# Three of fifteen streamed weight slices loaded as 108 and 20 rows

## The chip, the cores and the metric

The kernel runs on one core of a Trainium2 chip. Five engines work side by side on the core: PE (TensorE, the matmuls), ACT (ScalarE), DVE (VectorE), POOL (GpSimd) and SP (SyncE, which here only issues transfers). Sixteen DMA engines move data between the memory outside the core (HBM) and the on-chip memory (SBUF, 128 rows or "partitions"). The metric is the device time of one execution in microseconds (us); less is better. The median of three runs is given with the lowest and the highest.

## The reference, cut to what matters

Two attention layers work on the same input `x` of 2048 tokens by 640 features, and a gate per token mixes them. Layer A is recurrent: it takes the tokens in 64 segments of 32, puts 8 memory rows ahead of each, and the first 8 rows of its output are the memory of the next segment.

```python
for s in range(n_seg):                                  # 64 segments, one after the other
    h = jnp.concatenate([mem, xs], axis=1)              # 8 + 32 rows of 640
    q = jnp.einsum('btd,dhe->bhte', h, Wq)              # 32 heads of 192: 640 x 6144 weights
    k = jnp.einsum('btd,dhe->bhte', h, Wk)
    v = jnp.einsum('btd,dhe->bhte', h, Wv)
    ...                                                 # masked softmax over the 40 rows
    o = jnp.einsum('bhte,hed->btd', o, Wo)              # 6144 x 640 weights
    mem = o[:, :M, :].copy()
...
return g * a + (1 - g) * b                              # b: local dilated attention, not recurrent
```

So every segment needs all of `Wq`, `Wk`, `Wv` and `Wo` (31.5 MB in bf16), which is more than the on-chip memory holds, and no segment can start before the one ahead of it has its output.

## The kernel before

The kernel has three stages. `part_b` computes layer B and the gate (up to about 163 us of the span). `prepass` computes what of layer A does not depend on the memory (up to about 459 us). `part_a` then runs the 64 segments, and `part_z` finishes some output rows from 1880 us on.

**Slices.** The weights are cut into 80 slices of 128 rows by 1536 columns (384 KB): `("q", R, kc)`, `("k", R, kc)`, `("v", R, kc)` with R from 0 to 3 and kc from 0 to 4, and `("oa", i)` and `("ob", i)` for `Wo`. `weights_setup` (L339) spreads `N_STREAM = 15` of them evenly over an estimated segment; those are streamed, that is, loaded again in each segment. The other 65 stay in SBUF. In the order of use the streamed ones are q02, k04, q14, q20, k20, q30, k30, v0 (R 0, kc 0), v1, v2, v3, oa0, oa5, oa7 and ob4, where q14 stands for `("q", 1, 4)`.

**Loads.** `get_slice` (L390) gives back a resident tile, or calls `load_slice` (L374) for a tile of the pool `wstream`, tag `wst`, which has `WBUFS = 5` buffers. `load_slice` makes one transfer on SP's queue: from the weight itself (L382) or, for the four streamed slices of `Wo`, from a copy `wscr` in HBM that was rearranged once at the start (L380). A buffer's load can be issued when the matmuls on the slice five ahead of it are done. The scheduler of the framework puts the waits on semaphores in; for PE and ACT the order written out in `part_a` is kept (`manual_schedule`, L519). Transfers issued by SP and ACT take their completion semaphore in turn out of eight, and a transfer is issued only when the one that used its semaphore before has landed.

**A segment.** `m_qk` (L523) multiplies the 40 rows by a `q` or `k` group: five slices, four matmuls each, side by side on the columns of PE (L531). `t_qk` transposes (L545), `s_a` and `s_b` make the scores (L568, L577), `e_exp` and `e_norm` the softmax, `m_v` the values (L614), `pv_half` the weighted sum (L634, L638), `o_group` the product with `Wo` (L671), and `sel` (L681) picks the memory rows for the next segment. At the segment's end ACT copies the last results of `pv_half` (L644, L649), issues the next segment's loads `KZ` (L504) and `ZQ` (L505) and the store `oz_dram` (L732), and then copies the first part of the output (L739), from which `sel` starts the next memory. ACT issues four more transfers per segment: the store of the output rows (L764, 4 rows outermost), `Vz` (L510), `a4` (L715) and `hT` (L500). SP issues the 15 slices and nothing else there.

The 15 slices and these seven are the 22 transfers of a segment. `prepass` reads slices too; q14 and v0 are each streamed once more there. At the very end ACT stores the last segment's rows in four transfers of 24 rows (L767). In `part_b` the weight `wo_pad` is loaded in four transfers of 20 rows (L136).

Of the kernel before, what the change touches and what calls it, by code (L numbers as in the profile page):

```python
# [15 lines left out]
N_LATE = 55  # L16
N_LATE2 = 22
WBUFS = 5

_DEV = {"mode": "full"}  # L20

# [3 lines left out]
class _K:  # L25
# [313 lines left out]
    def weights_setup(self):  # L339
        nc, tc = self.nc, self.tc  # L340
        keys = self.slice_keys()
        gap = {("q", 0, 3): 200, ("k", 0, 3): 0, ("q", 1, 0): 620, ("k", 1, 0): 270, ("q", 2, 0): 570, ("k", 2, 0): 270,
               ("q", 3, 0): 980, ("k", 3, 0): 270, ("v", 0, 0): 690, ("v", 1, 0): 270, ("v", 2, 0): 710,
               ("v", 3, 0): 1160, ("oa", 6): 1530, ("q", 0, 0): 200}
        at, t = {}, 0
        for k in keys:
            t += gap.get(k, 0)
            at[k] = t
            t += 163
        self.stream_keys = set()  # L350
        for i in range(N_STREAM):
            left = [k for k in keys if k not in self.stream_keys]
            self.stream_keys.add(min(left, key=lambda k: abs(at[k] - (i + 0.5) * t / N_STREAM)))
        rest = [k for k in keys if k not in self.stream_keys]
        first = ["q", "k", "v", "oa", "ob"]
        self.late = sorted(rest, key=lambda k: first.index(k[0]))[-N_LATE:]
        self.wres = self.ctx.enter_context(tc.tile_pool(name="wres", bufs=1))
        self.res_tiles = {}
        self.wscr = {}
        self.early = [k for k in rest if k not in self.late]  # L360
        self.wstream = self.ctx.enter_context(tc.tile_pool(name="wstream", bufs=WBUFS))

# [11 lines left out]
    def load_slice(self, pool, key, name, tag=None):  # L374
        src, split = self.slice_info(key)
        kw = {"tag": tag} if tag else {}
        t = pool.tile([128, 1536], BF, name=name, **kw)
        v = t if split is None else t.rearrange("p (c f) -> p c f", c=split[0])
        if key in self.wscr:
            self.nc.sync.dma_start(t[:], self.wscr[key])  # L380
        else:
            self.nc.sync.dma_start(v[:], src)  # L382
        return v

    def load_late(self, part):
# [493 lines left out]
```

## Time and profile before

| | |
|---|---|
| time, median of 3 runs | 1916.34 us (1915.34 to 1916.49) |
| the profiled execution | 1921.93 us, span 1920.1 us |
| mean granted clock of PE in it | 0.981 |
| instructions | 91,285, of PE 41,135 matmuls and as many weight loads |
| stage `part_a` | 459 to 1880 us, 64 segments of about 22.4 us |
| PE busy in that stage | 1304.9 of 1421 us |
| slices streamed | 977 transfers of 384 KB, of them 960 in the segments |
| moved in all | 489.24 MB, 423.28 MB on SP's queue, 60.12 MB on ACT's |

The profile is that of one execution. Busy time is the time in which an engine had an instruction at work. A wait is the idle time of an engine ahead of an instruction, put down to what ended it: in a line such as `PE a <- DMA b: 21.7, 1, 21.7` the three numbers are microseconds in total, the number of waits, and the longest. The chain of waits is followed back from the last instruction, each time to what released it; "issue" in it is time in which the engine waited for nothing that the profile shows, and ACTq and SPq are the times in which ACT and SP issue transfers. In the table of stages each engine has its busy time and its instructions; the granted clock of PE, the mean busy share of the 16 DMA engines and the GB/s they moved follow. The queues are q1 (issued by SP), q10 (issued by ACT), and q8 and q14, which bring instructions. Beside this the trace has a record of every packet of a DMA engine (start, length, bytes, queue) and of every increment of a semaphore; a packet there is one row of a transfer, or a 4-byte increment.

### The profile page before, as it was taken

The page shows a single profiled execution, that of the slowest core. Times are in us where ns is not written, and L with a number is a line of the kernel's source. Part 1 is how long each engine was busy: PE and PEld are TensorE (multiplying, and loading weights), DVE is VectorE, ACT ScalarE, POOL GpSimd, SP SyncE. Part 2 cuts the span into 40 slices and gives each one's busy share as a digit, 9 for nine tenths or more (in the row PEclk, how much of TensorE's full clock was granted, in tenths as well). Part 3 has the DMA queues.
Part 4 walks back from the last instruction along what each step waited for, and adds up shares of the span by engine and source line. Part 5 has one row for each costly group of instructions (what it writes and reads, how often), then busy time and mean ns, then how long its engine had stood idle before and what let it go on. Part 6 is the DMA issues. An engine that isn't in the chain of part 4 may idle for free.

```text
span 1920.1 us, 91285 instructions
## 1 busy us (share of the span) xinstructions
PE 1727.8 (90%) x41135; PEld 1023.9 (53%) x41135; DVE 651.3 (34%) x2047; ACT 742.0 (39%) x1865; POOL 70.2 (4%) x135
## 2 busy tenths in 40 slices
PE   6898899957998999999999989898999999899979
PEld 3555544424555555555555555555555555555547
DVE  4555433212333333333333333333333333333320
ACT  3666522213433333334333334333333333343340
POOL 5000000000000000000000000000000000000000
PEclk9999899988999999999999999999999999999999
DMA  6610385689989999899999889888998899998981
GB/s 167 176 31 18 112 289 152 175 280 302 300 289 287 303 289 302 284 296 293 291 293 292 286 278 303 276 286 294 294 293 286 283 298 297 296 297 286 296 291 30
DMA packets 300298, 489.24 MB, mean 255 GB/s; under 512 B 99332, under 2 KB 168452, under 8 KB 299908
## 3 DMA queue, kind: packets, MB, share of 16 engines
q1 hardware_dynamic: 183544, 423.28, 67.2%
q10 hardware_dynamic: 116364, 60.12, 11.5%
q8 instruction: 322, 5.28, 1.1%
q14 instruction: 68, 0.56, 0.1%
HBM read 448.97 MB, written 35.91 MB: 253 GB/s over the span
## 4 chain that ended last, share of the span: by engine, by line
PE 75%; ACT 8%; issue 5%; DMA 4%; ACTq 4%; DVE 3%; SPq 1%; DVEq 0%
PE ps_qk L531 24%; PE ps_v L614 12%; PE ps_wo L671 7%; PE ps_qkT L545 6%; PE ps_pre L417 6%; PE ps_bqk L220 3%; PE ps_oT L634 3%; PE ps_S L568 3%; PE ps_z L811 3%; PE ps_pre L430 2%; ACT bP L243 2%; ACT KV L536 2%; ACTq L505 1%; DVE KV L644 1%; ACT ZQ L739 1%
## 5 line engine op out<-in xcount | busy, mean ns | idle before, releaser
L536 ACT CAST KV<-ps_qk 128x384 bf16<-128x384 f32 x512 | 238.6, 479 | 397.6 <-PE ps_qk L531 389.4
L531 PEld LDWEIGHTS <-hT 128*32 128x32 bf16 x10240 | 237.4, 96 | 177.0 <-issue 59.4
L531 PE MATMUL ps_qk<-wlate_k,hT 128*32 128x384 bf16 x4352 | 247.0, 328 | 1.5 <-issue 1.5
L614 PE MATMUL ps_v<-wlate_v,hT 128*32 128x384 bf16 x4096 | 227.9, 330 | 6.3 <-issue 6.1
L671 PEld LDWEIGHTS <-KV 128*32 128x32 bf16 x6144 | 171.9, 97 | 105.2 <-DVE KV L644 35.0
L531 PE MATMUL ps_qk<-wres_q,hT 128*32 128x384 bf16 x2560 | 163.3, 329 | 20.4 <-ACT KV L536 16.8
L548 DVE COPY ZQ<-ps_qkT 128x384 bf16<-128x384 bf16 x256 | 91.0, 355 | 262.9 <-PE ps_qkT L545 262.7
L671 PE MATMUL ps_wo<-wlate_oa,KV 128*32 128x384 bf16 x2304 | 158.6, 336 | 12.8 <-DVE KV L644 2.9
L614 PEld LDWEIGHTS <-hT 128*32 128x32 bf16 x5120 | 114.5, 96 | 93.4 <-DMA wst<-in_A_Wv_dram 21.8
L531 PE MATMUL ps_qk<-wst,hT 128*32 128x384 bf16 x1792 | 153.5, 330 | 5.5 <-DMA wlate_v<-in_A_Wv_dram 4.1
L545 PE MATMUL ps_qkT<-ident,KV 128*128 128x128 bf16 x1536 | 141.2, 221 | 3.4 <-DVE ZQ L607 1.4
L671 PE MATMUL ps_wo<-wlate_ob,KV 128*32 128x256 bf16 x2688 | 133.2, 279 | 10.3 <-issue 10.2
L644 DVE CAST KV<-ps_oT 128x192 bf16<-128x192 f32 x256 | 79.8, 352 | 181.9 <-ACT KV L644 181.8
L545 PEld LDWEIGHTS <-KV 128*128 128x128 bf16 x1536 | 87.8, 98 | 94.3 <-issue 93.7
L671 PE MATMUL ps_wo<-wst,KV 128*32 128x384 bf16 (+1 forms) x1152 | 124.4, 317 | 3.2 <-issue 2.5
L644 ACT CAST KV<-ps_oT 128x192 bf16<-128x192 f32 x256 | 69.8, 325 | 119.7 <-PE ps_oT L638 118.5
L614 PE MATMUL ps_v<-wst,hT 128*32 128x384 bf16 x1024 | 89.8, 337 | 23.2 <-DMA wst<-in_A_Wv_dram 21.7
L531 PE MATMUL ps_qk<-wlate_q,hT 128*32 128x384 bf16 x1536 | 109.0, 330 | 0.3 <-issue 0.3
L618 ACT CAST KV<-ps_v 128x384 bf16<-128x384 f32 x128 | 61.2, 478 | 107.8 <-DMA wst<-wscr 33.5
L568 PE MATMUL ps_S<-ZQ,KV 128*32 128x40 bf16 (+1 forms) x4096 | 99.2, 186 | 0.5 <-DVE KV L552 0.5
L684 DVE CAST hT<-ps_mem 128x24 bf16<-128x24 f32 x126 | 22.5, 178 | 222.5 <-PE ps_mem L681 222.5
L568 PEld LDWEIGHTS <-KV 128*32 128x32 bf16 (+1 forms) x4096 | 77.5, 92 | 37.3 <-DVE KV L552 0.9
(130 smaller groups left out, 2214.3 us busy)
## 6 DMA issues: line engine op xcount, KB each, us to landing
wst<-in_A_Wv_dram SPq DMA_DIRECT2D x266, 384.0 KB
wst<-in_A_Wq_dram SPq DMA_DIRECT2D x260, 384.0 KB
wst<-wscr SPq DMA_DIRECT2D x256, 384.0 KB
wst<-in_A_Wk_dram SPq DMA_DIRECT2D x195, 384.0 KB
zpk_dram<-ZS ACTq DMA_DIRECT2D x4, 3072.0 KB
ZQ<-zpk_dram ACTq DMA_DIRECT2D x128, 96.0 KB
wlate_k<-in_A_Wk_dram SPq DMA_DIRECT2D x17, 384.0 KB
wlate_v<-in_A_Wv_dram SPq DMA_DIRECT2D x16, 384.0 KB
```

The costliest lines, as they stand in the source:

```text
L220: nc.tensor.matmul(ps[:, 0:nn], lhsT=wqk[n][:, kc, 4 * g:4 * g + 4, :].rearrange("p h d -> p (h d)"), rhs=xT[:, kc, o0:o0 + nn], start=(kc ...
L417: nc.tensor.matmul(ps[:], lhsT=sls[kc][:, c0:c0 + 128], rhs=zT[:, kc, :], start=(kc == 0), stop=(kc == KC - 1))
L531: nc.tensor.matmul(pq[32 * j:32 * j + 32, 0:384], lhsT=hT[:, kc, :], rhs=sl[:, 384 * j:384 * j + 384], start=(kc == 0), stop=(kc == KC - 1 ...
L536: nc.scalar.copy(st, pq[:, 0:384])
L545: nc.tensor.transpose(pT[:, t, :, :, :].rearrange("p j b i -> p (j b i)"), st[:, 128 * t:128 * t + 128], self.ident[:])
L548: nc.vector.tensor_copy(q_blocks(R)[:, 1:5, :, :].rearrange("p b c i -> p c b i"), pT.rearrange("p t j b i -> p (t j) b i"))
L568: nc.tensor.matmul(pSs[h][32 * j:32 * j + 32, par, 40 * r:40 * r + 40], lhsT=KT[k0:k1, 12 * r + c, :], rhs=q_blocks(R)[k0:k1, :, c, :], st ...
L614: nc.tensor.matmul(pv[32 * j:32 * j + 32, 0:384], lhsT=hT[:, kc, :], rhs=sl[:, 384 * j:384 * j + 384], start=(kc == 0), stop=(kc == KC - 1 ...
L618: nc.scalar.copy(V[R], pv[:, 0:384])
L634: nc.tensor.matmul(out[:, r, t, :], lhsT=V[2 * h + r][ks, f0:f1], rhs=E[ks, par, 40 * r:40 * r + 40], start=(r == 0 and t == 0), stop=Fals ...
L644: cp(oTxs[2 * h + j // 2][:, 6 * (j % 2):6 * (j % 2) + 6, :], pos[j // 2][:, j % 2, 0:240].rearrange("p (c q) -> p c q", q=40)[:, :, 8:40])
L671: nc.tensor.matmul(pso[part][32 * jj:32 * jj + 32, 0:n], lhsT=oTxs[2 * (R // 2) + j // 2][:, 6 * (j % 2) + 3 * (R % 2) + t, :], rhs=o_weig ...
```

## The change

Of the 15 streamed slices the three at places 2, 7 and 12 of the order of use (counted from 0: q14, v0 and oa5) are loaded by two transfers, one of 108 rows and one of 20, instead of one of 128. The bytes, the buffer, the matmuls and their order stay as they are. All other loads through `load_slice` keep one transfer of 128 rows.

```diff
+SPLIT_ROWS = 108
+SPLIT = (2, 7, 12)
...
             self.stream_keys.add(min(left, key=lambda k: abs(at[k] - (i + 0.5) * t / N_STREAM)))
+        order = [k for k in keys if k in self.stream_keys]
+        self.split_keys = [order[i] for i in SPLIT]
...
         v = t if split is None else t.rearrange("p (c f) -> p c f", c=split[0])
-        if key in self.wscr:
-            self.nc.sync.dma_start(t[:], self.wscr[key])
-        else:
-            self.nc.sync.dma_start(v[:], src)
+        cuts = (0, SPLIT_ROWS, 128) if tag and key in self.split_keys else (0, 128)
+        for r0, r1 in zip(cuts, cuts[1:]):
+            if key in self.wscr:
+                self.nc.sync.dma_start(t[r0:r1, :], self.wscr[key][r0:r1, :])
+            else:
+                self.nc.sync.dma_start(v[r0:r1], src[r0:r1])
         return v
```

## The prediction

> **What bounds the kernel now.** I read the page's first parts, then the busy time by stage, the waits, the chain of waits in a late segment, and last the trace's own records of DMA packets and semaphore increments, because the change touches nothing but transfers.
>
> ```profile
> PE 1727.8 (90%) x41135; PEld 1023.9 (53%) x41135; DVE 651.3 (34%) x2047; ACT 742.0 (39%) x1865; POOL 70.2 (4%) x135
> ...
> q1 hardware_dynamic: 183544, 423.28, 67.2%
> ...
> q8 instruction: 322, 5.28, 1.1%
> ...
> PE 75%; ACT 8%; issue 5%; DMA 4%; ACTq 4%; DVE 3%; SPq 1%; DVEq 0%
> ```
>
> PE carries 75% of the chain, DMA 4%. Two small entries matter here: "issue" 5% (96 us) and ACTq 4% (77 us), time in which PE or ACT waits for no data. The recurrent part fills 1420 us of the span, 64 segments of about 22.4 us:
>
> ```profile
> 459.00:1880.00 1421.00, 1304.91 (x35922) 789.16 (x35918) 467.42 (x1706) 551.13 (x1516) 31.44 (x62) 0.99 0.90 290
> ```
>
> The last three columns are clock 0.99, DMA share 0.90 and 290 GB/s. That looks like a DMA bound, but the waits point the other way:
>
> ```profile
> PE ps_v L614 <- DMA wst<-in_A_Wv_dram: 21.7, 1, 21.7
> ...
> SPq L382 <- PE ps_qk L531: 405.9, 373, 2.2
> SPq L382 <- PE ps_wo L671: 225.1, 226, 4.0
> ```
>
> PE waited once for a slice; SP waits hundreds of times for PE to release one of five buffers. From the trace: a load is issued 0.05 us after its buffer's last matmul, its last increment comes 4.5 us later (median), and the slice's first matmul later still. That margin has medians of 3.6 us for the third slice of a segment (q14), 2.2 us for the eighth (v0) and 1.6 us for the thirteenth (oa5), the three that are split; 17 of their 192 margins are under 1 us.
>
> So what could a transfer's shape change? The chain shows it:
>
> ```profile
> 978.14 0.13 PE ps_oT L634
> 978.28 1.22 issue
> 979.50 0.25 PE ps_oT L634 x15
> ...
> 981.07 1.60 ACTq L505
> ...
> 983.19 0.49 ACT ZQ L739
> ```
>
> **First,** PE stands still for 1.22 us between two matmuls of one line. Counting PE's instructions, this is at a multiple of 256 from the last such stop. Queue q8 moved 322 packets of 16 KB, and PE's 82,270 instructions make 321 blocks of 256: q8 brings PE's code. Of 282 block boundaries in the recurrent part 77 show PE idle over 0.1 us, together 63.8 us, and PE resumes 1.26 to 1.59 us after the packet ended. **Second,** ACT needs 1.60 us to issue the transfer of L505, which usually takes 0.45. Of the 60 issues of SP and ACT over 0.7 us, 53 ended 0.18 to 0.40 us after the end of a code packet: I read this as one DMA engine that takes no further descriptors while a code packet (median 0.97 us) holds it.
>
> Which engine is it? A transfer's increments tell how many engines it uses: 16 for 128 rows, 10 and one for the rest for 20 rows (`wo_pad`), 12 and one for 24 rows (the last stores, L767), 4 and one for 4 rows: each time the largest divisor up to 16. During the code packet of 1879.84 to 1880.88 us, two of those 12-engine stores did all their 48 packets and wrote all 24 increments. So the code engine is none of the 12. Nine times all four increments of a four-engine transfer fell inside a code packet too, while of the 16-engine loads never more than 15 did.
>
> **The change part by part.** By the same divisor 108 rows go to 12 engines, 9 rows each, and 20 rows to 10 engines, 2 each. *Assuming that the 12 are the same 12*, the code engine gets nothing of three slices in 15: 96 rows a segment instead of 120 (-20%); ten engines get 129 (+7.5%), two 123. [...]
>
> *Code fetch (gain).* A code packet starts 1.94 us (median) after PE enters the block before the one it brings. In the last 40 us of the span, where the DMA share is 0.10, it starts at -0.06 us: the difference, 2.0 us, is load. A fit over the 278 fetches gives 1.26 us plus 0.087 us for each row waiting on an engine, 8.2 rows on average (correlation 0.41). 20% less is 1.6 rows, 0.14 us. On 77 stops that is 11 us. Ends: 0 if the relieved moments miss the stops; 20% of 2.0 us, 0.40 x 77 = 31 us, if all the delay is load. I take 11, from the fit, because it is measured on this queue. A stopped PE has nothing queued that could go ahead, and ACT and DVE wait behind it; so I count it in full. The next limit is the ACT chain at the segment's end.
>
> *ACT's issue (gain).* L505 takes 0.605 us on average against a median of 0.446 (62 times: 9.9 us), L732 0.484 against 0.383 (63 times: 6.4 us). Both stand in the chain just ahead of the copy at L739. Four transfers are typically under way there (k04, q14, KZ, q20), and q14 is now off the code engine. Ends 0 and 16 us; I take a third, 5 us, since one of the three full loads is gone.
>
> *PE's waits (cost).* A matmul pair carries two waits, one on its weight load and one on the matmul. q14 and oa5 use one today, so their second fits. v0 uses both, so a separate semaphore instruction is added: 51 ns in the trace's three per segment. 64 x 51 ns = 3 us; ends 0 (PE's queue is ahead) and 10 us if all three slices need one. I take 3.
>
> *Landing (cost).* Ten engines do 11 rows instead of 8, at 118 ns each by the packets' starts: +0.35 us; the second issue on SP adds 0.33 us ahead of its 2 rows. With the split slices 0.5 us later, the margins of all 64 segments lack 0.5 us in sum. If all 15 slices came 0.36 us later it would be 1.4 us. I take 0; the ends are -1 us (the code engine is often the last to land, 0.48 us after the fifteenth) and the slower rival below.
>
> *SP and semaphores.* Three more issues, 1 us per segment of a queue that waits about 1000 us for PE; the next release comes 0.8 us later or more. Eight semaphores are used in turn by all transfers of SP and ACT, and each issue waits for the one eight before. With 25 instead of 22 per segment I moved the pairing along on the old times: of some 1,475 pairs six are short, by at most 0.24 us (ACT's L505 and L732). Under 1 us; taken as 0.
>
> Sum: -11 - 5 + 3 = **-13 us**. The profiled execution took 1921.93 us (its span 1920.1 and 1.8 around it) and becomes 1908.9. The median shown, 1916.34, is 5.6 us lower, so I predict **1903.3 us**.
>
> [...]
>
> **The rivals.** *No relief (0.17).* Either the 12 engines of a load are not the 12 of a store, or 108 rows are spread otherwise: then code fetch and issue stay, and only 0 to 3 us are added: 1916 to 1919. For it: the fit explains little of the spread. Against it: the divisor held for every row count present. *Slower (0.16): the split slices come late.* Place: oa5 and v0, the small margins. The second transfer is handed over separately and can itself wait for a code packet (q14's issue reaches 1.88 us, mean 0.50), and ten engines carry 7.5% more. From the margins: 1 us later costs 4 us, 1.5 us costs 16, 2 us costs 43; it decides from about 1.5 us. With half of the gains left, 16 - 8 + 3 gives about 1927. Against it: 0.35 to 0.7 us is all that the rows support. *Full relief (0.12).* Both upper ends, 31 + 16 - 3 = 44 us: 1872; more likely some 30: 1886. For it: a fetch that finds its engine empty saves far more than the mean.
>
> **How the numbers follow.** My forecast has 0.55, with a range of its own of 1892 to 1911. The three others hold 0.45. A measurement tells 0.2%, 3.8 us, from no change, so "faster" is below 1912.5: 0.55 and 0.12, less a little for the forecast's edge: 0.65. "Same" is the no-relief case and that edge: 0.19. "Slower": 0.16. The range of 8 in 10 leaves out the lower half of full relief and the larger part of the slower case: 1884 to 1922.
>
> **What would show it.** Right: the 108-row load leaves 13 increments, the 20-row load 11; PE's stops at block boundaries fall from 63.8 to about 53 us and the code packet's start from 1.94 to about 1.8 us; L505 and L732 together lose 5 us of issue; oa5 and v0 keep margins over 0.3 us; one semaphore instruction more per segment on PE. Wrong: stops unchanged, or a new wait of PE for `wst` at L614 or L671 of several us in sum.

## The result, and the profile after

The changed kernel takes **1980.82 us** (median of 4 runs, 1969.04 to 1983.28), the kernel before beside it 1916.41: the ratio is 1.031 [1.0266, 1.0355]. It is 64 us slower, where 13 us faster was predicted, and above the stated range of 1884 to 1922. The profiled execution took 1983.15 us with a span of 1981.3. Lines of the code lie 2 to 6 further down: L531, L614, L634, L671, L505 and L732 are now L537, L620, L640, L677, L511 and L738, and the loads of L380 and L382 are L386 and L388.

The page of the changed kernel, engines, queues and chain:

```profile
PE 1755.7 (89%) x41120; PEld 1034.8 (52%) x41135; DVE 651.6 (33%) x2047; ACT 743.7 (38%) x1865; POOL 70.3 (4%) x135
...
q1 hardware_dynamic: 184708, 423.28, 67.8%
...
q8 instruction: 322, 5.28, 1.1%
...
PE 71%; DMA 8%; ACT 8%; issue 6%; ACTq 3%; DVE 2%; SPq 1%; DVEq 0%
```

The bytes on q1 are the same to the last digit. In the chain DMA rises from 4% to 8% and issue from 5% to 6%, and PE falls from 75% to 71%. The table of stages for the recurrent part, which now ends at 1941 us:

```profile
459.00:1941.00 1482.00, 1333.35 (x35936) 800.56 (x35932) 468.45 (x1707) 552.73 (x1516) 31.58 (x62) 0.97 0.90 279
```

This one line holds half of the answer. The stage is 61 us longer (1482 against 1421). PE is *busy* 28.4 us more (1333.35 against 1304.91) on the same matmuls, and its clock is 0.97 instead of 0.99; the other 32.6 us it stands idle. The DMA share stays at 0.90 while the rate falls from 290 to 279 GB/s: the engines are as busy as before and move less. Where PE stands idle, from its waits, first before:

```profile
PEld L634 <- issue: 45.5, 94, 1.8
PEld L671 <- issue: 24.3, 39, 2.5
...
PEld L614 <- issue: 14.4, 31, 2.0
```

and after:

```profile
PEld L640 <- issue: 64.0, 122, 3.7
...
PEld L677 <- issue: 40.7, 81, 2.3
...
PEld L620 <- issue: 26.8, 47, 4.4
...
PEld L677 <- DMA wst<-wscr: 11.6, 18, 1.3
```

PEld is the weight load, one to a matmul (41,135 of each); L634, L671 and L614 of before are L640, L677 and L620 now. The three waits grow by 12 to 19 us each, and the profile shows nothing that PE waits for in them; the table below counts how much of this is PE waiting for its code. The fourth line is new: oa5, and a little oa0, land too late. And the waits of SP's queue:

```profile
SPq L388 <- DMA wst<-in_A_Wq_dram: 34.6, 44, 3.0
...
SPq L388 <- DMA a<-bsc_dram: 21.7, 29, 1.3
SPq L388 <- DMA wst<-in_A_Wk_dram: 21.4, 25, 2.0
```

An issue of SP now often waits for an earlier transfer, whose completion semaphore it needs. In the recurrent part SP's waits of this kind at the loads grew from 20 (34 us) to 146 (128 us).

From the trace's records, segments only (a "long packet" is one of 3072 bytes that took over 130 ns, 600 to 1800 us of the trace; "stops" are PE's idle times over 0.1 us at code blocks; "half clock" is time at half speed from the start of the first segment to the start of the last; "slice waits" are PE's waits for a streamed slice, without one of 22 to 23 us for v0 in the first segment, which both kernels have):

| | before | after |
|---|---|---|
| issue to last increment, q14 / v0 / oa5 | 4.7 / 4.0 / 4.4 us | 6.1 / 5.2 / 5.9 us |
| the same, whole slices q02 / k04 / oa0 | 4.2 / 4.5 / 4.7 us | 4.8 / 5.5 / 5.7 us |
| margin of v0 / oa5 (median) | 2.2 / 1.6 us | 1.2 / 0.6 us |
| long packets | 10.3% | 28.6% |
| stops at code blocks | 64 us | 95 us |
| half clock | 44 us in 7 pieces | 113 us in 24 |
| slice waits | 0 | 11 us in 35 |

**How a stop becomes two losses.** The chain of the changed kernel, and its profile in four stretches of 3.41 us, around one stop. 3.41 us is the step of the clock's own record: all of its pieces but the last, at full and at half speed, are whole multiples of it, before and after. One step is called a clock window here.

```profile
978.91 1.89 issue
980.80 0.22 PE ps_oT L640 x6
```

```profile
974.66:978.08 3.42, 3.40 (x106) 2.15 (x106) 1.72 (x5) 1.53 (x5) 0.00 (x0) 1.00 0.93 327
978.08:981.49 3.41, 1.52 (x70) 0.86 (x66) 0.34 (x2) 0.83 (x4) 0.00 (x0) 1.00 0.92 280
981.49:984.90 3.41, 3.41 (x96) 1.93 (x88) 1.70 (x6) 0.95 (x5) 0.00 (x0) 0.56 0.68 170
984.90:988.32 3.42, 3.30 (x83) 2.16 (x82) 0.97 (x4) 1.26 (x4) 0.00 (x0) 0.94 0.86 248
```

PE stands still for 1.89 us in the second stretch (busy 1.52 of 3.41), and half speed follows. The clock's own record has it from 981.9 to 985.3 us, 0.4 us later than the third stretch, which therefore reads 0.56 and the fourth 0.94. Two of the 24 half-speed pieces lie in the first segment; each of the other 22 follows a clock window with 1.2 to 2.7 us of idle time. Not every such window is followed by half speed. In the 16 profiles of whole kernels together, from 450 us on and window by window, half speed came after 3 of 6,016 full-speed windows with less than 1.2 us idle, 31 of 186 with 1.2 to 1.5, 66 of 103 with 1.5 to 1.8, and 86 of 95 with more. By these windows a matmul stream that is late by 1.9 us mostly loses up to another 1.7 us, half of 3.41. No window counted above was idle from end to end (at most 3.21 us of 3.41).

**The account closes.** Between the first and the last segment the profiled execution is 63.5 us longer. PE's gaps over 0.1 us grew by 34.2 us (stops by about 30 and slice waits by 11, while the others fell), and half of PE's busy time in half-speed windows, an estimate of what the clock cost, grew by 30.9 us: 65.1 in sum.

### The profile page after: what moved, and what is told of

Its sections match the earlier page's. It is cut to its first block, busy times and chain, and to the rows that moved or that the text cites. A ratio compares the mean times of both kernels' runs of the same rounds, so it can differ in the third digit from the quotient of the medians.

```text
span 1981.3 us, 91467 instructions
## 1 busy us (share of the span) xinstructions
PE 1755.7 (89%) x41120; PEld 1034.8 (52%) x41135; DVE 651.6 (33%) x2047; ACT 743.7 (38%) x1865; POOL 70.3 (4%) x135
## 4 chain that ended last, share of the span: by engine, by line
PE 71%; DMA 8%; ACT 8%; issue 6%; ACTq 3%; DVE 2%; SPq 1%; DVEq 0%
PE ps_qk L537 23%; PE ps_v L620 10%; PE ps_wo L677 8%; PE ps_qkT L551 6%; PE ps_pre L423 5%; DMA wst<-wscr 4%; PE ps_bqk L222 3%; PE ps_z L817 3%; PE ps_oT L640 3%; PE ps_S L574 2%; ACT bP L245 2%; PE ps_pre L436 2%; ACT KV L542 2%; DMA wst<-in_A_Wv_dram 1%; ACTq L511 1%
## 5 line engine op out<-in xcount | busy, mean ns | idle before, releaser
L537 PEld LDWEIGHTS <-hT 128*32 128x32 bf16 x10240 | 238.3, 96 | 181.6 <-issue 63.7
L537 PE MATMUL ps_qk<-wlate_k,hT 128*32 128x384 bf16 x4352 | 249.3, 329 | 5.0 <-issue 5.0
L677 PEld LDWEIGHTS <-KV 128*32 128x32 bf16 x6144 | 179.7, 102 | 131.7 <-issue 40.7
L620 PE MATMUL ps_v<-wlate_v,hT 128*32 128x384 bf16 x4096 | 231.7, 333 | 7.2 <-issue 7.0
L677 PE MATMUL ps_wo<-wlate_oa,KV 128*32 128x384 bf16 x2304 | 170.6, 359 | 14.2 <-issue 8.3
L537 PE MATMUL ps_qk<-wres_q,hT 128*32 128x384 bf16 x2560 | 163.9, 331 | 18.1 <-ACT KV L542 16.6
L620 PEld LDWEIGHTS <-hT 128*32 128x32 bf16 x5120 | 116.0, 97 | 107.8 <-issue 26.8
L537 PE MATMUL ps_qk<-wst,hT 128*32 128x384 bf16 x1792 | 153.6, 331 | 5.0 <-ACT KV L542 3.2
L677 PE MATMUL ps_wo<-wlate_ob,KV 128*32 128x256 bf16 x2688 | 140.3, 291 | 7.7 <-issue 7.7
L677 PE MATMUL ps_wo<-wst,KV 128*32 128x384 bf16 (+1 forms) x1152 | 125.1, 337 | 16.5 <-issue 8.9
L620 PE MATMUL ps_v<-wst,hT 128*32 128x384 bf16 x1024 | 91.1, 339 | 33.8 <-DMA wst<-in_A_Wv_dram 23.3
L537 PE MATMUL ps_qk<-wlate_q,hT 128*32 128x384 bf16 x1536 | 109.6, 332 | 1.0 <-issue 1.0
L640 PE MATMUL ps_oT<-ZQ,KV 32*128 32x40 bf16 (+1 forms) x4096 | 72.2, 187 | 31.7 <-issue 31.3
```

The costliest lines, as they stand in the source:

```text
L537: nc.tensor.matmul(pq[32 * j:32 * j + 32, 0:384], lhsT=hT[:, kc, :], rhs=sl[:, 384 * j:384 * j + 384], start=(kc == 0), stop=(kc == KC - 1 ...
L620: nc.tensor.matmul(pv[32 * j:32 * j + 32, 0:384], lhsT=hT[:, kc, :], rhs=sl[:, 384 * j:384 * j + 384], start=(kc == 0), stop=(kc == KC - 1 ...
L640: nc.tensor.matmul(out[:, r, t, :], lhsT=V[2 * h + r][ks, f0:f1], rhs=E[ks, par, 40 * r:40 * r + 40], start=(r == 0 and t == 0), stop=Fals ...
L677: nc.tensor.matmul(pso[part][32 * jj:32 * jj + 32, 0:n], lhsT=oTxs[2 * (R // 2) + j // 2][:, 6 * (j % 2) + 3 * (R % 2) + t, :], rhs=o_weig ...
```

## The experiments

Theories. **Rows:** a transfer whose rows are not spread over the DMA engines as 128 rows are makes packets long, its own and those beside it. **Load:** ten engines have 11 rows instead of 8, by the prediction's count from the increments; the records name no engines. **Second transfer:** issuing and landing two transfers costs. **Margins:** slices simply land too late. Two came later: **ports**, a more exact form of *rows* (it matters which rows of the on-chip memory a transfer writes; that rows share ways into it is the author's guess at the cause), and the one **PE instruction** per segment that the split of v0 brings.

### Which part of the split

e1_columns, the three slices as two transfers of 128 rows:

```diff
+        cuts = (0, 768, 1536) if tag and key in self.split_keys else (0, 1536)
+        for c0, c1 in zip(cuts, cuts[1:]):
...
+                self.nc.sync.dma_start(t[:, c0:c1], (self.wscr[key] if key in self.wscr else src)[:, c0:c1])
```

> The same three slices are loaded in two transfers each, but cut by columns: 128 rows by 768 columns twice, so all 16 engines take 8 rows of each. Three theories of the loss of 64 us. Rows (my theory now): a transfer whose rows are not 128 is laid over the DMA engines so that its packets and those served beside it take longer; in the trace of after, 51% of the 3072-byte packets served during a 108-row load take 130 to 400 ns, against 12% at other times and 6.5% before. It expects 1916 to 1930 here, with slow packets as before. Load (rival): ten engines do 11 rows instead of 8; it expects 1916 to 1930 too. Second transfer (rival): the additional issue, wait and turn of a semaphore cost by themselves; it expects about 1980.

Measured 1921.03 us, 1.0029 [0.9996, 1.0061]; long packets 10.7%, stops 57 us, half clock 41 us. As many transfers as the changed kernel, and nothing measurable lost: *second transfer* falls.

e2_112_16 has `SPLIT_ROWS = 112`: by the same count 16 engines with 7 rows, then 16 with one.

> 112 and 16 rows instead of 108 and 20: by the divisor 16 engines take 7 rows and then 1, so every engine has 8 rows of each slice as before, but not the rows it had. Rows: slow, 1950 to 2000, with over 12% of the packets between 130 and 400 ns. Load: 1916 to 1930. Second transfer: about 1980, with the packets as quick as before. Together with the columns this tells all three apart.

Measured 1958.67 us, 1.0213 [1.0161, 1.0264]; long packets 24.8%, stops 92 us, half clock 72 us. By that count no engine has more rows than before, and two thirds of the loss remain, so a loss of this kind doesn't need *load*. How much *load* adds in 108+20 this run doesn't tell, because 112+16 has longer packets of its own, as the transfers alone will show.

e5_108only loads 108 rows of the three slices in the segments and multiplies only those:

```diff
+        cuts = (0, SPLIT_ROWS) if tag and key in self.split_keys and self.cut else (0, 128)
...
+                            nc.tensor.matmul(pq[32 * j:32 * j + 32, 0:384], lhsT=hT[0:n, kc, :],
+                                             rhs=sl[0:n, 384 * j:384 * j + 384], start=(kc == 0), stop=(kc == KC - 1),
```

> In the segments the three slices get their 108-row transfer only; the other 20 rows are neither loaded nor multiplied there, so part of three products is left out. One transfer per slice as before, no engine has more than 9 rows, and the total is 3% less. Rows: still slow, 1940 to 1980, most of the slow packets stay. Load: 1905 to 1925. Second transfer: 1905 to 1925. If the code engine is really relieved and nothing is slowed, 1890 to 1905.

Measured 1934.45 us, 1.0088 [1.0054, 1.0121]; long packets 21.8%, stops 62 us, half clock 65 us, slice waits 8 us. Less than theory *rows* expected, and more than the others did: the 108 rows alone, without the other 20, cost 17 us by the ratio, with no engine above 9 rows by the count. The rest of the loss comes with the 20 rows, which are both a second short transfer and, by the count, two more rows for ten engines; no run takes these two apart.

e4_early has `SPLIT = (0, 1, 2)`, where the margins were 2.7 us and more.

> 108 and 20 rows again, but for the first three slices of a segment (q02, k04, q14), which before had median margins of 2.7, 2.8 and 3.6 us. If the loss comes by PE waiting for the slices with small margins (oa5, oa0, v0), it falls to a fifth or less: 1920 to 1935, although the packets are as slow as after. If it comes in another way (ACT's transfers, code fetch), it stays near 1980, or grows, since ACT's own loads follow these three.

Measured 1945.14 us, 1.0148 [1.01, 1.0196]; long packets 20.7%, stops 79 us, slice waits 8 us, of them 7 at q14, whose margin had been 3.6 us. Between the two expectations: place matters, and margins are not the whole.

### Transfers alone

m1_loads and m2_rows have no matmuls, only stretches of 40 slices through the same five buffers. The loop of m1, whose `cuts` are rows or columns:

```python
def load(i, cuts):
    t = pool.tile([128, 1536], BF, name="wst", tag="wst")
    for r, c in cuts:
        nc.sync.dma_start(t[r, c], src[i % 20][r, c])
```

> Transfers alone: 13 stretches of 40 slices each through five buffers on SP's queue, in each one shape, no matmuls (the three products, the softmax and the output are left out; the output is zeros). Order: 128 rows; 108+20; 112+16; 120+8; 64+64; even and odd rows; two halves of the columns; 108 alone; 112 alone; 120 alone; 64 alone; 128 again; one 108+20 among four of 128. Theory rows (packets slow where the rows of a transfer are not spread over the engines as 128 are, eight neighbouring rows to each): 128 rows, 120 and even/odd near 0.12 us a packet, so about 1.0 to 1.3 us a slice; 108+20, 112+16, 64+64 and 108, 112, 64 alone 20 to 100% longer per packet. Theory load (ten engines have 11 rows): packets as long in every stretch, 108+20 about 11/8 of the time of 128 rows, 112+16, 64+64 and 120+8 at most 9/8. Theory crowd (packets slow only beside the kernel's other traffic): all stretches within 15% per byte.

The table of stretches of m1_loads, each from the landing of its tenth slice to that of its last; the last three columns are clock, DMA share and GB/s. In order: 128 rows, 108+20, 112+16, 120+8, 64+64, even and odd rows, two halves of the columns, 64 alone (upper half), 128 again.

```profile
22.60:52.70 30.10, 0.00 (x0) 0.00 (x0) 1.00 1.01 387
68.30:116.20 47.90, 0.00 (x0) 0.00 (x0) 1.00 0.79 256
129.60:171.00 41.40, 0.00 (x0) 0.00 (x0) 1.00 1.03 285
186.10:233.00 46.90, 0.00 (x0) 0.00 (x0) 1.00 0.95 256
248.40:296.80 48.40, 0.00 (x0) 0.00 (x0) 1.00 1.04 246
308.80:347.30 38.50, 0.00 (x0) 0.00 (x0) 1.00 0.93 307
357.70:389.50 31.80, 0.00 (x0) 0.00 (x0) 1.00 1.05 369
562.10:590.90 28.80, 0.00 (x0) 0.00 (x0) 1.00 0.98 211
600.40:630.00 29.60, 0.00 (x0) 0.00 (x0) 1.00 1.03 401
```

Here is the disputed cost by itself. 30 slices of 128 rows take 30.1 us; as 108+20 rows they take 47.9 us, at 256 instead of 387 GB/s. In 112+16, 120+8 and 64+64 the engines are busy (0.95 to 1.04) and still move 26 to 36% less: packets of one and the same 3072 bytes take 173, 173 and 208 ns (median) instead of 121. 108+20 has both handicaps: packets of 136 ns, and a share of 0.79, which fits the prediction's count of ten engines with 11 rows and the others with fewer. By that count theory *load* is right here: 11 rows instead of 8 would by themselves make 1.38 us of the 1.00 us a slice, so in this one shape, alone, they would be the larger part of what is added, and the longer packets the rest. In the other three, where by the same count no engine has more than 9 rows, *load* explains little. *Rows* is right for the packets but was wrong in one guess: 120 rows, thought to lie as eight neighbouring rows to an engine like 128, are as slow as the others (179 ns alone). And 64 rows of the upper half (rows 0 to 63) need 0.96 us, nearly as long as 128.

> Transfers alone again: 12 stretches of 40, no matmuls (the products, the softmax and the output are left out; the output is zeros). Order: 128 rows; rows 0 to 63; rows 32 to 95; even rows; 64 neighbouring source rows into the even rows; even source rows into rows 0 to 63; rows 0 to 31; rows 0 to 95; rows 32 to 127; a slice in even and odd rows, each from 64 neighbouring source rows; a slice in four transfers of 384 columns; 128 rows again. [...] Theory half (64 rows in one transfer are slow wherever they lie): rows 32 to 95 as rows 0 to 63, 0.9 us or more. Theory source (the reads of HBM set it): the two mixed stretches follow the source rows and not the rows written. [...]

m2_rows, same columns. In order: 128 rows, rows 0 to 63, rows 32 to 95, even rows, 64 neighbouring source rows into even rows, even source rows into rows 0 to 63.

```profile
21.40:51.60 30.20, 0.00 (x0) 0.00 (x0) 1.00 1.04 391
60.70:89.30 28.60, 0.00 (x0) 0.00 (x0) 1.00 1.01 208
95.90:117.60 21.70, 0.00 (x0) 0.00 (x0) 1.00 0.85 272
124.50:146.30 21.80, 0.00 (x0) 0.00 (x0) 1.00 0.84 274
153.10:175.40 22.30, 0.00 (x0) 0.00 (x0) 1.00 0.86 270
184.80:212.80 28.00, 0.00 (x0) 0.00 (x0) 1.00 1.00 207
```

Rows 0 to 63 and rows 32 to 95 are the same number of rows, by the count on the same number of engines. The first take 242 ns a packet, twice 121; the second 121 ns. Where 64 rows are *written* decides: neighbouring rows written to even rows are fast, even rows written to rows 0 to 63 slow (239 ns), each at the rate of the place written (270 GB/s beside 274 for even rows, 207 beside 208 for rows 0 to 63). The stretches of 64 rows that are not slow took 0.72 to 0.74 us a slice. So theory *ports* holds for these shapes in what it says of the times: the rows written decide, and rows 0 to 63 move at 208 GB/s, about half the 391 of 128 rows, while rows 32 to 95 move at 272. Its guess that rows share ways in was not shown: no run has a record of such ways. Three stretches that the table leaves out belong here. Rows 0 to 31 move at 205 GB/s, as rows 0 to 63 do, though in packets of 121 ns. Rows 0 to 95 take 1.17 us a slice and rows 32 to 127 take 1.14 us, in packets of 199 and 193 ns, longer than whole slices of 128 rows at 1.00. So 96 rows are slow too, though rows 32 to 127 contain the fast rows 32 to 95; why, no run shows. Which engine writes which rows no run shows either. For 108+20 and 112+16 the runs show only that the packets take longer (136 and 173 ns instead of 121); that the rows written are the cause there too is an inference from m2.

### The same shapes inside the kernel

e6_even_odd and e7_halves split the same three slices in two times 64 rows (`t[0::2]` and `t[1::2]`; `SPLIT_ROWS = 64`); e8_120_8 has `SPLIT_ROWS = 120`.

> The three slices in two transfers of 64 rows, the even and the odd rows. Both use 16 engines with 4 rows each. Theory rows: if an engine has eight neighbouring rows of a 128-row load, it has four of the same eight here, nothing is spread anew, and the time is 1912 to 1930, with 10 to 14% of the long packets over 130 ns. Theory count (any transfer of fewer than 128 rows slows): 1950 to 2000 with 25% or more.

> The three slices in two transfers of 64 rows, the upper and the lower half. As many transfers, engines and rows per engine as with even and odd rows; only which rows an engine has differs. Theory rows: 1950 to 2010, 25% or more of the packets over 130 ns. Theory load (uneven engines): even here, so 1912 to 1930. Theory count: as with even and odd rows, within 10 us of it.

> The three slices as 120 and 8 rows: by the divisor rule seen so far 15 engines with eight rows each, which are the same rows as in a 128-row load, and 8 engines with one row. Theory rows: 120 rows do no harm, the 8 rows (one row an engine, elsewhere) a little: 1910 to 1935, 11 to 16% of packets over 130 ns. Theory count: 1950 or more. The theory of the prediction, that one engine left out of three loads frees the code fetch, would show here without the harm: code stops under 55 us and 1900 to 1912.

Measured: e6 1942.45 us, 1.0115 [1.0051, 1.0179], long packets 11.5%, stops 94 us; e7 1986.13 us, 1.033 [1.0267, 1.0393], 31.1%, 93 us; e8 1968.57 us, 1.0233 [1.0177, 1.0288], 30.0%, 89 us. e7 and e6 differ in nothing but which rows each transfer has: 44 us. e8 missed its range because 120 rows are slow by themselves, as m1 shows; the engine that by the count its 120 rows leave free brings nothing that shows. e6 missed its range too, by 12 us, with few long packets. That opened a question: e6's stops were as many as those of the changed kernel.

### Repeats, single slices, and the added instruction

r_after is the changed kernel once more; e9_q14 has `SPLIT = (2,)`, e10_oa5 `SPLIT = (12,)`.

> The changed kernel once more, for a second profile beside the next two on one chip. All theories: ratio 1.025 to 1.037. Whether the sums of one profile carry the account: code stops 85 to 105 us and half-speed time 85 to 140 us between the first and the last segment if they do.

> Only q14 as 108 and 20 rows. Its margin was 3.6 us, so no matmul waits for it. Theory rows (slow packets, then late code packets, stops, half clock): a third of the long packets added, 15 to 18% over 130 ns, and a third of the loss without the waits: 1925 to 1940. Theory margins (the loss comes from slices that land too late): within 0.3% of before.

> Only oa5 as 108 and 20 rows. Its margin was 1.6 us, the smallest. Theory rows: as with q14 alone plus its waits, 1930 to 1948, 15 to 18% over 130 ns. Theory margins: most of the 64 us, 1950 to 1975.

Measured: r_after 1968.56 us, 1.0293 [1.0227, 1.0359], stops 90 us, half clock 92 us; e9 1929.94 us, 1.0054 [1.0012, 1.0096], long packets 15.2%, no slice waits to speak of (0.2 us); e10 1942.71 us, 1.0153 [1.0093, 1.0213], 19.0%, slice waits 13 us. One slice with a wide margin still costs 10 us by the ratio; the one with the smallest margin costs 29. Neither is most of the loss: *margins* falls as the whole cause and stays as a part.

All kernels with stops of 89 us and more (after, r_after, e2, e6, e7, e8) split v0 by rows, and there PE has 64 semaphore instructions more (261 instead of 197). Those without (e4, e5, e9, e10) have 60 to 79 us. Four kernels tell the two apart. x1_cut320 is e1 with its cut at column 320, so that the first matmul needs both transfers and v0 gets the instruction; x2_v1 and x3_eo_v1 split v1 instead of v0 (`SPLIT = (2, 8, 12)`), by 108+20 and by even and odd rows; x4_nop adds `nc.tensor.nop(nofuse=True)` to the kernel before, ahead of v0.

> As e1_columns, in two transfers of 128 rows, but cut at column 320, so that the first matmul on each of the three slices (columns 0 to 383) needs both transfers. For v0 that makes a separate semaphore instruction on PE, 64 in all, as the changed kernel has; for q14 and oa5 there is room on the pair. No transfer has fewer than 128 rows. Theory PE instruction (the added instruction moves PE's code blocks against the segment, or holds PE's sequencer, and code stops rise with it): 1930 to 1950, ratio 1.007 to 1.02, code stops 80 to 95 us, long packets as before. Theory ports alone: within 0.4% of before, stops 57 to 65 us.

> 108 and 20 rows as in the changed kernel, but of q14, v1 and oa5 instead of q14, v0 and oa5. The first matmul on v1 has one wait, so a second finds room and no instruction is added. Theory PE instruction and ports: long packets 25 to 29%, code stops 65 to 80 us instead of 90 to 95, 1935 to 1952. Theory ports alone: as the changed kernel, 1962 to 1985 with stops over 85 us.

> Even and odd rows of q14, v1 and oa5. Neither long packets nor an added instruction: theory PE instruction and ports: within 0.5% of before, stops 55 to 70 us. If even and odd rows cost something of their own: 1.008 to 1.015 as with v0.

> The kernel before, with one empty instruction on PE ahead of v0 in each segment (64 in all). It waits for nothing; it only moves PE's code blocks against the segment as the added semaphore instruction does. If the place of the block boundaries makes the stops: stops 80 to 95 us, 1930 to 1950, as x1_cut320. If it is the wait in an instruction of its own that does (the sequencer runs less far ahead): within 0.4% of before, stops 55 to 68 us, while x1_cut320 is slower.

Measured: x1 1922.41 us, 1.0024 [0.9996, 1.0052], with 261 semaphore instructions and stops of 71 us; x2 1970.46 us, 1.0275 [1.0247, 1.0304], with 197 and stops of 82 us; x3 1941.03 us, 1.0134 [1.0081, 1.0187], with 197 and 69 us. *PE instruction* falls: with it and no slow rows the loss is at most 10 us and not clear of none, without it and with slow rows it is nearly all there. x4 (1921.12 us, 0.9992 [0.9961, 1.0022]) tells nothing on this: its stops lie at the same multiple of 256 from start to end, so the empty instruction was not in PE's stream. It serves as a second profile of the kernel before (stops 61 us, half clock 58 us).

### All together

| split of the three slices | alone, us a slice | GB/s in the kernel | ratio |
|---|---|---|---|
| columns (e1) | 1.06 | 261 | 1.0029 |
| even and odd rows (e6; with v1: x3) | 1.29 | 246; 249 | 1.0115; 1.0134 |
| 112+16 (e2) | 1.37 | 243 | 1.0213 |
| 120+8 (e8) | 1.55 | 241 | 1.0233 |
| 108+20 (after; r_after; with v1: x2) | 1.58 | 236; 238; 233 | 1.031; 1.0293; 1.0275 |
| 64+64 (e7) | 1.61 | 235 | 1.033 |

The second column is m1's time per slice (128 rows: 1.00). The third is what SP's queue moved from 1.5 us after the issue of a split slice to its landing; before, the same three slices whole give 260. The more a shape costs by itself, the more the kernel loses. This puts even and odd rows in their place as well: few of their packets are over 130 ns, but some are very long (5% over 281 ns in m1), and by rate they lie between columns and 112+16. One run doesn't fit the third column: x1, which loses nothing measurable, moves only about 250. So the order rests on the second.

How the profiled executions' longer stage divides, each less the kernel before (PE's gaps over 0.1 us; half of its busy time at half speed):

| | stage | gaps | clock | sum |
|---|---|---|---|---|
| after | +63.5 | +34.2 | +30.9 | 65.1 |
| r_after | +46.1 | +26.2 | +22.3 | 48.5 |
| e7_halves | +64.3 | +39.9 | +27.5 | 67.4 |
| e8_120_8 | +51.0 | +29.8 | +21.2 | 51.0 |
| e2_112_16 | +42.0 | +24.0 | +12.9 | 36.9 |
| e10_oa5 | +18.8 | +10.1 | +9.6 | 19.7 |
| e9_q14 | +13.2 | +7.5 | +3.8 | 11.3 |
| x2_v1 | +57.5 | +35.5 | +20.1 | 55.6 |
| e6_even_odd | +35.5 | +21.7 | +18.2 | 39.9 |
| e4_early | +26.9 | +20.6 | +0.2 | 20.8 |
| x1_cut320 | +11.9 | +6.6 | +1.8 | 8.4 |

Half to two thirds of most losses is idle time, and the rest is the clock that the idle time costs. In e4 the clock cost nothing: its half-speed time was 48 us, against 44 before. Two profiles of one kernel differ by 17 us, and x1, whose time is not clear of that of before, was profiled in an execution with a stage 12 us longer. So one row's split is good to some 10 us, and the smallest rows show little.

## Why the prediction was wrong

**The step that failed is the landing term,** "Ten engines do 11 rows instead of 8, at 118 ns each by the packets' starts". The 118 ns were the packets of 128-row transfers. The term was then taken as 0, because 0.5 us fits into the margins. The trace of before had no transfer of 108 rows beside others, and the cost of a shape that it does not show was taken from one that it shows and bounded by counting rows. Alone, 108+20 takes 1.58 us a slice instead of 1.00; 11/8 would be 1.38. In the kernel the split slices land 1.1 to 1.5 us later, not 0.35 to 0.5, and the slices beside them 0.2 to 1.0 us later. The second half of the step, that a late landing costs only where a margin ends, failed as well: PE's waits for slices are 11 of the 64 us, and the larger part came by way of the code and the clock, as follows.

**Code fetch, predicted -11 us, was about +30.** A stop follows a simple sum: the end of the code packet, plus 1.40 us, less the time that PE needs for the block ahead. Over all blocks this gives 63.0 us for the kernel before (63.1 in the same blocks of the trace) and 94.3 after (95.0). The packet ends on average only 0.12 us later (3.06 to 3.18 us after PE enters the block), but the latest 3% move from 4.35 to 4.78 us, and the added stops are made there. By a slightly wider count of the stops (69 and 99 us), the packets that end over 4 us after PE's entry went from 22 to 44 of 279, and the stops behind them from 13 to 46 us, while those behind the earlier packets stayed at 56 and 52. That slower transfers make the code packets late fits all runs, but no run changed the one without the other. The twelve-engine reading may hold: the transfers left 13 and 11 increments, as predicted, but no record has an engine's number. Whether it relieves the code's engine was not shown. In e5, with 20 rows less, packets start at 1.91 instead of 2.00 us, and its stops (62 us) hardly fall.

**ACT's issue, predicted -5 us, rose:** L511 takes 0.74 us on average (0.61 before), L738 0.51 (0.48). That is some 10 us over the segments on ACT; what it cost the whole was not measured.

**PE's added wait, predicted +3 us,** is right in what it adds, one semaphore instruction per segment (261 instead of 197 in all). Its price stays open: the interval of x1, -1 to +10 us, includes 3 and 0.

**SP and semaphores, "under 1 us; taken as 0":** moving the pairing along on the old landing times missed that landings themselves get later. SP waited 146 times instead of 20. Their price apart from the rest was not measured, but their number doesn't order the losses: e1 has 66 such waits (61 us) and loses nothing measurable, e9 103 (95 us) and loses 10 us, e4 302 (355 us) and loses 28 us, the changed kernel 146 and loses 64.

**The clock was not in the sum at all.** A stop was priced at its own length; in the account above the added idle time of 34.2 us cost 65.1 with the clock, nearly twice that. The rival "Slower", with 0.16, had the right sign and place (oa5), and its price for the waits was about right: 4 to 16 us for 1 to 1.5 us of delay, 11 us measured. The sign that the prediction named for it, a new wait for `wst` at L671 (now L677), came with 11.6 us. But it priced only these waits, kept half of the gains beside them, and so came to 1927.

## What to carry to other kernels

Keep a load at 128 rows (1.00 us a slice alone), and where it must be cut, cut it once by columns (1.06 us alone, the kernel at 1.0029). The cuts at rows 64, 108, 112 and 120 were slow by themselves (1.61, 1.58, 1.37 and 1.55 us), the one at 112 although by the count no engine has more rows than before, and in the changed kernel whole slices beside the cut ones landed 0.2 to 1.0 us later. Measure a transfer's shape by itself before pricing it from another shape's packets. And where PE is the bound, look for clock windows with over 1.5 us of idle time: 152 of 198 were followed by 3.41 us at half speed, which by an estimate (half of 3.41) can cost up to 1.7 us more.

## What the runs showed of the hardware that was not expected

- 64 rows cost 0.95 us a slice in rows 0 to 63 and 0.72 us in rows 32 to 95; the rows written decide it, not the rows read (64 neighbouring rows into even rows took 0.74, even rows into rows 0 to 63 0.93).
- 108 rows in one transfer alone move at 1.39 us a slice, longer than 128 rows at 1.00.
- Idle time of over 1.8 us in one 3.41 us clock window was followed by half speed in the next in 86 of 95 cases, 1.2 to 1.5 us in 31 of 186, and less in 3 of 6,016.
- A slice in four transfers of 384 columns took 1.90 us in m2, against 1.06 in two: I read this as the eight completion semaphores used in turn, which leave only two such slices under way; that was not tried apart.
